# Seven half-size block products for the feature transform of three chunks: an FNet and MLP kernel on one Trainium2 core

## The chip, the cores and the metric

The kernel runs on one core of one Trainium2 chip. The metric is the device time of one execution in microseconds, and lower is better. Engines go by the names of the profile: PE is TensorE (matmuls; PEld is its loading of weights), DVE is VectorE, ACT is ScalarE, POOL is GpSimd, SP is SyncE, which here only issues DMA transfers. Each engine runs its own instructions in order and waits for others by semaphores.

## The reference

The input x has 2048 tokens of 512 features. Four steps run in turn, A, B, A, B; the kernel calls the first A and B layer 0, the second pair layer 1. Cut to what matters here:

```python
def _A_ref(x, dft_seq_re, dft_seq_im, dft_hid_re, dft_hid_im):
    a = jnp.einsum("bsd,ed->bse", x, dft_hid_re)
    b = jnp.einsum("bsd,ed->bse", x, dft_hid_im)
    return jnp.einsum("ts,bse->bte", dft_seq_re, a) - jnp.einsum("ts,bse->bte", dft_seq_im, b)

x = A_x
x = x + _A_ref(_layernorm(x), ...)      # layer A
x = x + _B_ref(_layernorm(x), ...)      # spatial shift and MLP, untouched here
x = x + _A_ref(_layernorm(x), ...)
x = x + _B_ref(_layernorm(x), ...)
```

Step A is a discrete Fourier transform over the tokens and one over the features, of which the real part is kept. The order of the two can be exchanged, and the kernel does the tokens first.

## The kernel before

**Precision.** Every product is done in fp32r, with each operand split into a high and a low part. `mm3` (L315) issues three matmuls per product: high x high (L316), high x low (L317), low x high (L318). The high part is a rounding copy on ScalarE, the low part a subtraction on VectorE.

**Work.** Each of the two A steps handles its 2048 output tokens in four chunks of 512 (NC = 4, `c`). For a chunk, an x phase (`x_phase`, L498) and a y phase (`y_phase`, L531) do the transform over tokens with sums (`ax`) and differences (`ay`) of the normalised input as stationary operand and the DFT matrix `ws` as moving operand, 512 columns at a time, into the PSUM pairs PA, PB, PC, PD. Out come four tiles of features by tokens, `re0`, `re1`, `im0`, `im1`, kept as high and low parts in the region `rr`. The first chunk of layer 0 goes by another routine, `plain_phase` (L456).

**The transform over features** of chunk c - 1 is done inside the x phase of chunk c, by `hid` (L593): eight calls a chunk, two passes over the four blocks of the DFT matrix `hs` (order `HORDER`, L42), each with 2 x 2 products of 128 x 128 by 512 columns into PD. The list `HAT` (L40) puts the calls ahead of the steps k = 2, 3, 3, 4, 5, 5, 6, 6. After four calls `add_y` (L609) adds PD onto two tiles of x (X1) on VectorE, and `y_stats` (L618) takes their statistics. The last chunk's transform runs after the loop over chunks.

**Feeding.** A list `pieces` (L180) of 512 KB blocks is loaded by SP in order into four raw buffers (`issue_dma`, L235; RAW = 4): piece i goes into buffer i mod 4, and waits until the users of piece i - 4 are done. A list `items` (L184) names what TensorE streams, in order. `stage_one` (L247) makes the high part of an item in one of four ring slots (RING = 4): a cast of a plain block on ScalarE (L260), or a difference on VectorE (L262, L266) and then its cast (L263, L267). `stage_two` (L272) makes the low part on VectorE (L279). `stream()` (L304) takes the next item: it frees the slot of the item before, issues the first stage of as many items as have a slot, one low part behind, and returns the slot. In an x phase, each step k has a plain item (12 matmuls) and a "one" item (6); each y item has 12.

**Order around the change.** Everything is issued by hand (`manual_schedule`). `late` is a table of small jobs; `run_late(i)` (L493) issues those of half-step i = 2k or 2k + 1 right behind `stream()` and ahead of that item's matmuls. `hook(i)` does the same for row transfers. In `by_pairs`, which does step B, `D(slot, ...)` and `A(slot, ...)` put jobs on VectorE or ScalarE into numbered slots; at L1050 two sums of z3 blocks stand in slot 26.

Of the kernel before, what the change touches and what calls it, by code (L numbers as in the profile page):

```python
# [40 lines left out]
BACK = {8: 0, 9: 2}  # L41
HORDER = ((1, 0), (0, 1), (1, 1), (0, 0))  # L42


@with_exitstack
def spectral_mlp_kernel(ctx: ExitStack, tc: tile.TileContext, x, ws, hs, w1, w2, w34, out, out_t):
# [40 lines left out]
    EXT = RNG + RING * 4 * CH  # L87
    RAWS = EXT + 6 * D
    STG = RAWS + RAW * 2 * CH
    nc.alloc_sbuf_tensor("arena", [P, STG + 2 * CH], F32)  # L90

# [22 lines left out]
    spare = at("spare", SPARE, 2, D, dtype=F32)  # L114
    (re0, im0), (re1, im1) = ([both(f"rr{i}{h}", RR + (2 * i + h) * 4 * CH, 2, 2, CH) for i in range(2)] for h in range(2))
    rr = [[re0[0], re1[0]], [im0[0], im1[0]]]
    rg = [[at(f"rg{i}{g}", RR + (4 * i + g) * 2 * CH, 2, CH) for g in range(KD)] for i in range(2)]
    ring, ringf = zip(*(both(f"ring{i}", RNG + i * 4 * CH, 2, 2, CH) for i in range(RING)))
# [68 lines left out]
    def y_order():  # L187
        order = [(k, kind) for k in range(NP) for kind in ("by1", "by0")]
        order[-3], order[-2] = order[-2], order[-3]
        return order  # L190

    for layer in range(LAYERS):
        for c in range(NC):
            if layer == 0 and c == 0:
                for k in range(NP):
                    item("plain", piece(ws[c, k][:, 2:4]))
                    item("plain", piece(ws[c, k][:, 0:2]))
                continue
            for k in range(NP):
                if c:  # L200
                    for h in range(NP):
                        if HAT[h] == k:
                            item("plain", piece(hs[HORDER[h % 4]]))
                p = piece(ws[c, k][:, 2:4])
                item("plain", p)
                item("one", p, span=(0, 1))
            ps = [(piece(ws[c, k][:, 2:4]), piece(ws[c, k][:, 0:2])) for k in range(NP)]
            for k, kind in y_order():
                item(kind, *ps[k])
        for o in HORDER:  # L210
            item("plain", piece(hs[o]))
        w_items.append(len(items))
        for i in range(2):
            item("plain", piece(w1[i]), dest=w12[i])
        for i in range(2):
            item("plain", piece(w2[i]), dest=w12[2 + i])
        w_pieces.append(len(pieces))
    users = {}
    for n, it in enumerate(items):
        for i in it[1]:  # L220
            users.setdefault(i, []).append((n, "two" if it[0] == "plain" else "one"))
    raws, slots, sums = {}, {}, {}
    state = {"dma": 0, "one": 0, "two": 0, "use": 0, "made": 0, "done": 0, "limit": 0, "load": w_pieces[0]}
# [11 lines left out]
    def issue_dma(upto=None):  # L235
        while state["dma"] < (state["load"] if upto is None else upto):
            i = state["dma"]
            if i >= RAW and any(n >= state[stage] for n, stage in users[i - RAW]):
                break
            src, a, b = pieces[i]  # L240
            raws[i] = raw_at[i % RAW]
            nc.sync.dma_start(raws[i][:, a:b], src)
            state["dma"] += 1
            if i % 2 and i > 3:
                load_x()
# [198 lines left out]
    re0s, re1s, im0s, im1s = (f[:, :, 1] for _, f in (re0, re1, im0, im1))  # L444
    mid = [rr[i // 2][i % 2].rearrange("p t r (h d) -> p (t r h) d", h=2) for i in range(4)]
    mid = [m[:, 0:4].rearrange("p (i r) d -> p i r d", r=2) for m in mid]

# [8 lines left out]
    def plain_phase(hook):  # L456
# [19 lines left out]
        for (t, _), ps, sign in ((im0, PC, -1.0), (re1, PB, 1.0)):  # L476
            for i in range(2):
                nc.scalar.mul(t[:, i, 0], ps[i], sign)
                nc.vector.scalar_tensor_tensor(
                    t[:, i, 1], ps[i], sign, t[:, i, 0].bitcast(F32), op0=ALU.mult, op1=ALU.subtract  # L480
                )
        for t, ps, sign in ((re0s, PA, 1.0), (im1s, PD, -1.0)):
            for i in range(2):
                nc.scalar.mul(t[:, i], ps[i], sign)
        late[2] = [lambda: high(im1)]
# [7 lines left out]
    def run_late(*names):  # L493
        for i in names:
            for f in late.pop(i, ()):
                f()

    def x_phase(c, hook):  # L498
        h = 0
        for k in range(NP):  # L500
            first, last = k == 0, k == NP - 1
            while c and h < NP and HAT[h] == k:
                s = stream()
                ri, dp = HORDER[h % 4]
                hid(ri, dp, s, PD, 2 * (h // 4), h % 4 == 0, h % 4 == 3)
                if h % 4 == 3:
                    add_y(c - 1, h // 4, PD, X1, 2 * k if h < 4 else 2 * k + 2 if c == NC - 1 else "y")
                hook(NT + h)
                h += 1
# [5 lines left out]
            if last:  # L515
                for i in range(2):
                    nc.scalar.copy(im1s[:, i], PC[i])
                for i in range(2):
                    nc.scalar.copy(re1s[:, i], PB[i])
            s = stream()  # L520
# [3 lines left out]
        for i in range(2):  # L524
            nc.scalar.copy(re0s[:, i], PA[i])

# [4 lines left out]
    def y_phase(c, hook):  # L531
        im = pairs[1] if c == NC - 1 else im0s

# [4 lines left out]
        for k, kind in y_order():  # L538
            first, last = k == 0, k == NP - 1
            s = stream()  # L540
            if kind == "by1":
# [5 lines left out]
                if k == 6 and c == NC - 1:  # L547
                    add(pairs[0], re0s, re1s, ALU.subtract)
                jobs = (PC, ay[k][:, 2], s[:, 0]), (PD, ay[k][:, 0], s[:, 1])
                for job in jobs[::-1] if first else jobs:  # L550
                    mm_half(*job, first, last)
                if last:
                    for i in range(2):
                        nc.vector.scalar_tensor_tensor(
                            im[:, i], PC[i], -1.0, im1s[:, i], op0=ALU.mult, op1=ALU.subtract
                        )
                    nc.scalar.copy(im0[0][:, :, 0], im)
                    if c == NC - 1:
# [3 lines left out]
                    else:  # L562
                        x1_copies()
                    add(im1s, pairs[0] if c == NC - 1 else re0s, im)
            else:
                if k == NP - 2 and c < NC - 1:
                    im0_low(im)
# [7 lines left out]
        for i in range(2):  # L575
            nc.scalar.copy(t[:, 2 + i], PA[i])
        late.update(
            {
                "im1-": [lambda: add(im1s, im1s, re1s, ALU.subtract)] if c < NC - 1 else [],
                "re1+": [lambda: add(re1s, re1s, t[:, 0:2]), lambda: high(re1)],  # L580
                "im1+": [lambda: add(im1s, im1s, X1), lambda: high(im1)],
                "re1": [lambda: low(re1)],
                "re0+": [lambda: add(re0s, re0s, t[:, 0:2])],
                "im1": [lambda: low(im1)],
                "re0++": [lambda: add(re0s, re0s, t[:, 2:4]), lambda: high(re0)],
                "re0": [lambda: low(re0)],
            }
        )
        if c < NC - 1:
            for i, names in enumerate((["im1-"], ["re1+"], ["im1+", "re1"], ["re0+", "im1"], ["re0++"], ["re0"])):  # L590
                late[i + 1] = [f for n in names for f in late.pop(n)]

    def hid(ri, dp, s, acc, t0, first, last):  # L593
        for i in range(2):
            for t, a in enumerate(acc):
                w = slice((t0 + t) * P, (t0 + t + 1) * P)
                mm3(
                    a,
                    rr[ri][dp][:, i, 0, w],
                    rr[ri][dp][:, i, 1, w],  # L600
                    s[:, i, 0],
                    s[:, i, 1],
                    first and i == 0,
                    last and i == 1,
                )
# [231 lines left out]
    def by_pairs(layer, zs, xin, dst):  # L837
# [739 lines left out]
    for layer in range(LAYERS):  # L1577
        xin = x if layer == 0 else x2d
        last_layer = layer == LAYERS - 1
        state["limit"] = w_items[layer]  # L1580
        zs = {}
        for c in range(NC):
            if layer == 0 and c == 0:
                raws[0] = raw_at[0]
                load_x()
# [76 lines left out]
            def hook(i):  # L1662
                k, odd = divmod(i, 2)
                if layer == 0 and c == 1:
                    if i == 1:
                        xp_sums(NP - 1)
# [4 lines left out]
                if c == 0:  # L1671
# [5 lines left out]
                    return  # L1677
                j = (c - 1) * TC
                if i == 4:
                    rows(X1, xin, j, 2, True)  # L1680
# [4 lines left out]
                if c == NC - 1:  # L1685
# [9 lines left out]
                    if i in (14, 15):  # L1695
                        turn_out(turn0, queue=nc.scalar, which=[i - 14])

            x_phase(c, hook)

            def hook(k):  # L1700
                if layer and c == 0 and k == 3:
                    xp_lows(NP - 1, which=slice(1, None))
                if k == 1 and c:
                    rows(X1, x1d, (c - 1) * TC + 2, 2, False)
                if c == NC - 1:
# [94 lines left out]
```

## Time and profile before

| | |
|---|---|
| median of 3 runs | 1429.36 us (1428.56 to 1430.61) |
| profiled execution | 1430.81 us |
| its span, first to last instruction | 1428.8 us |
| busy: PE / DVE / ACT / POOL | 1422.0 / 1147.5 / 726.3 / 79.9 us |
| granted PE clock | 1.0 in the whole span |
| DMA | 302.13 MB, 211 GB/s on average |

A row of the time order reads: start, length, engine, line, operation, what is written and read, sizes; in brackets the idle time of the engine before it and what ended it. A matmul's length is modelled and overlaps the next one's; its pace is read from the starts. A row of a window reads: stretch, its length, busy time of each engine with the number of instructions, PE clock, DMA share and GB/s.

### The profile page before, as it was taken

What the parts mean: (1) busy time and instruction counts of PE and PEld (TensorE: products, weight loads), DVE (VectorE), ACT (ScalarE), POOL (GpSimd) and SP (SyncE); (2) the same over time, 40 slices, a digit from 0 to 9 for tenths busy, and PEclk for the clock granted to TensorE, in tenths of its full rate; (3) what the DMA queues carried; (4) which work ended last, traced back from release to release, by engine and by line L of the source; (5) the groups of instructions that cost most, each with busy time, mean ns of one, the idle gap of its engine ahead of it and who ended that gap; (6) DMA issues with size and microseconds to landing.
All of it is one profiled execution on the core that took longest, in us unless ns stands there. A gap on an engine that the chain in (4) does not pass through costs nothing.

```text
span 1428.8 us, 17276 instructions
## 1 busy us (share of the span) xinstructions
PE 1422.0 (100%) x6258; PEld 1174.2 (82%) x6258; DVE 1147.5 (80%) x1603; ACT 726.3 (51%) x977; POOL 79.9 (6%) x111
## 2 busy tenths in 40 slices
PE   9999999999999999999999999999999999999998
PEld 7888888888888888888888888888888888888887
DVE  7876997988869888677889979888889698637586
ACT  5553454455465745345554544544555576333352
POOL 2100000001002000000000000000000010000000
PEclk9999999999999999999999999999999999999999
DMA  7426646657664859968755566565676468666594
GB/s 243 140 89 207 206 166 203 204 167 245 225 205 111 287 201 321 379 215 319 240 174 195 168 191 204 186 199 190 205 258 225 137 164 303 209 196 260 168 312 144
DMA packets 136813, 302.13 MB, mean 211 GB/s; under 512 B 15372, under 2 KB 61196, under 8 KB 133528
## 3 DMA queue, kind: packets, MB, share of 16 engines
q1 hardware_dynamic: 132504, 298.93, 63.1%
q10 hardware_dynamic: 4224, 2.10, 0.5%
q8 instruction: 49, 0.80, 0.2%
q14 instruction: 36, 0.29, 0.1%
HBM read 246.18 MB, written 54.81 MB: 211 GB/s over the span
## 4 chain that ended last, share of the span: by engine, by line
PE 95%; DVE 3%; DMA 2%; issue 0%; SPq 0%; ACT 0%; DVEq 0%
PE psd L318 10%; PE psd L316 10%; PE psd L317 10%; PE psa L316 9%; PE psa L318 9%; PE psa L317 9%; PE psc L317 6%; PE psc L318 6%; PE psc L316 6%; PE psb L317 6%; PE psb L318 6%; PE psb L316 6%; DMA raw<-in_ws 1%; DVE ring L279 1%; DMA xs<-in_x 1%; DVE ring1f L266 0%
## 5 line engine op out<-in xcount | busy, mean ns | idle before, releaser
L260 ACT CAST ring<-raw 128x1024 fp32r<-128x1024 f32 x127 | 133.0, 1052 | 98.9 <-PE psd L318 50.1
L279 DVE TENSOR_TENSOR ring<-raw,ring 128x1024 fp32r<-128x1024 f32 (+1 forms) x128 | 154.5, 1211 | 22.5 <-ACT ring L260 22.4
L316 PE MATMUL psd<-ring,rr 128*128 128x512 f32 x208 | 80.9, 389 | 0.0
L317 PE MATMUL psd<-ring,rr 128*128 128x512 f32 x208 | 80.9, 389 | 0.0
L318 PE MATMUL psd<-ring,rr 128*128 128x512 f32 x208 | 80.9, 389 | 0.0
L360 POOL TENSOR_TENSOR rs<-ve,mhalf 128x4 f32<-128x4 f32 x16 | 28.7, 1794 | 578.2 <-DVE nm L359 578.2
L267 ACT CAST ring<-ring0f 128x1024 fp32r<-128x1024 f32 x28 | 29.5, 1054 | 57.1 <-DVE ring0f L266 57.1
L279 DVE TENSOR_TENSOR ring<-ring1f,ring 128x512 fp32r<-128x512 f32 (+1 forms) x56 | 53.2, 949 | 0.8 <-ACT ring L263 0.8
L339 POOL TENSOR_TENSOR rs<-ve,mhalf 128x2 f32<-128x2 f32 (+1 forms) x33 | 30.1, 911 | 396.3 <-DVE nb L338 396.3
L317 PE MATMUL psc<-ring,ay 128*128 128x512 f32 x128 | 50.0, 391 | 0.9 <-DVE ring L279 0.9
L317 PE MATMUL psb<-ring,ay 128*128 128x512 f32 x128 | 50.1, 392 | 0.0
L318 PE MATMUL psc<-ring,ay 128*128 128x512 f32 x128 | 49.8, 389 | 0.0
L318 PE MATMUL psb<-ring,ay 128*128 128x512 f32 x128 | 49.8, 389 | 0.0
L316 PE MATMUL psb<-ring,ay 128*128 128x512 f32 x128 | 49.8, 389 | 0.0
L316 PE MATMUL psc<-ring,ay 128*128 128x512 f32 x128 | 49.8, 389 | 0.0
L267 ACT CAST ring<-ring1f 128x1024 fp32r<-128x1024 f32 x28 | 29.5, 1055 | 39.6 <-DVE ring1f L266 39.6
L317 PE MATMUL psa<-ring,ay 128*128 128x512 f32 x126 | 49.0, 389 | 0.0
L316 PE MATMUL psa<-ring,ay 128*128 128x512 f32 x126 | 49.0, 389 | 0.0
L318 PE MATMUL psa<-ring,ay 128*128 128x512 f32 x126 | 49.0, 389 | 0.0
L316 PE MATMUL psd<-ring,ay 128*128 128x512 f32 x126 | 49.0, 389 | 0.0
L317 PE MATMUL psd<-ring,ay 128*128 128x512 f32 x126 | 49.0, 389 | 0.0
L318 PE MATMUL psd<-ring,ay 128*128 128x512 f32 x126 | 49.0, 389 | 0.0
(575 smaller groups left out, 4375.4 us busy)
## 6 DMA issues: line engine op xcount, KB each, us to landing
raw<-in_ws SPq DMA_DIRECT2D x183, 512.0 KB, 4.9
raw<-in_hs SPq DMA_DIRECT2D x56, 512.0 KB, 3.6
w3b<-w3d SPq DMA_DIRECT2D x15, 1792.0 KB, 9.2
w4r<-w4a SPq DMA_DIRECT2D x33, 512.0 KB, 6.0
wq<-w4a SPq DMA_DIRECT2D x22, 512.0 KB, 4.7
w3d<-w3b SPq DMA_DIRECT2D x5, 1792.0 KB, 6.9
x1d<-tmp SPq DMA_DIRECT2D x12, 512.0 KB, 5.8
xs<-x1d SPq DMA_DIRECT2D x12, 512.0 KB, 6.6
```

What stands on the lines that cost most here:

```text
L260: nc.scalar.copy(dest[:, a:b, 0], r[0][:, a:b])
L267: nc.scalar.copy(dest[:, :, 0], lo)
L279: nc.vector.tensor_tensor(lo[:, i], src[:, i], hi[:, i].bitcast(F32), op=ALU.subtract)
L316: nc.tensor.matmul(o, lh, rh, start=first, stop=False, skip_group_check=onto)
L317: nc.tensor.matmul(o, lh, rl, start=False, stop=False, skip_group_check=onto)
L318: nc.tensor.matmul(o, ll, rh, start=False, stop=last, skip_group_check=onto)
L339: nc.gpsimd.tensor_tensor(rs[:, :n], ve[:, :n], mhalf[:, 0, :n], op=ALU.pow)
L360: nc.gpsimd.tensor_tensor(rs, ve, mhalf[:, :, :2], op=ALU.pow)
```

## The change

For three chunks (`by_seven`: the transforms done in the x phases of chunk 2 in layer 0 and of chunks 1 and 2 in layer 1) the 512 x 1024 by 1024 x 512 product becomes seven products of half size, in the manner of Winograd's variant of Strassen's scheme. Each unit (`hid_unit`) has 24 matmuls of 256 columns. The seven moving operands do not depend on the data of the chunk, so they are made once: three of them are stored out of ring slots during the first `hid` calls (layer 0, chunk 1), four are computed in the same x phase (`h_prep`), and all are kept in DRAM (`hd`, 1 MB each) with both parts. The stationary operands are sums and differences of the chunk's own tiles, made by VectorE and ScalarE in the half-steps of `plan_hid`, where the results are collected too. The statistics of the first two tiles and the sum and statistics of the last two move into the y phase (`x1b`). Two raw buffers serve as the buffer `hw[0]` meanwhile, so some pieces (`narrow`) use the other two alone; the region RAWS moves behind STG. The tiles in `rr` are laid out as quarters. Apart from that, one of the two z3 sums goes from slot 26 to slot 27.

```diff
+HUNITS = {3: (0,), 4: (1,), 5: (2,), 6: (3, 4), 7: (5, 6)}
+    hd = [dram.tile([P, KD, 2, 2 * P], F32, name=f"hd{i}") for i in range(7)]
...
+    quarter, quarterf = both("rr", RR, 2, 2, KD, 2, 2 * P)
+    first_diff, first_difff = both("fdiff", EXT, KD, 2, 2 * P)
+    hw = [at("hwa", RAWS + 4 * CH, KD, 2, 2 * P), at("hwb", EXT + 4 * CH, KD, 2, 2 * P), quarter[:, 1, 0]]
+    x1b = at("x1b", RR, 2, D, dtype=F32)
...
+    def by_seven(layer, c):
+        return 1 - layer < c < NC - 1
...
-                if c:
+                if c and not by_seven(layer, c):
                     for h in range(NP):
                         if HAT[h] == k:
                             item("plain", piece(hs[HORDER[h % 4]]))
...
+        j = min(range(2 if i in narrow else RAW), key=lambda j: last_in[j])
...
     def x_phase(c, hook):
+            if seven:
+                for u in HUNITS.get(k, ()):
+                    hid_unit(u)
-            while c and h < NP and HAT[h] == k:
+            while c and not seven and h < NP and HAT[h] == k:
                 s = stream()
                 ri, dp = HORDER[h % 4]
                 hid(ri, dp, s, PD, 2 * (h // 4), h % 4 == 0, h % 4 == 3)
+                if len(at_layer) == 1 and c == 1 and h < KD:
+                    for u, e in ((2, 0), (5, 1)) if h > 1 else ((0, 0),):
+                        v = s.bitcast(F32)[:, :, :, e * 2 * P : (e + 1) * 2 * P]
+                        nc.sync.dma_start(hd[u][:, h % 2 * 2 : h % 2 * 2 + 2], v)
...
+    def h_prep():
...
+        return {
+            2: [load(0), load(1)],
+            3: [load(2), load(3)],
+            5: [total(b22, b12, b22, ALU.add)],
+            6: [total(s2, b22, b11), hi(p, s2)],
+            7: [total(b21, b21, s2)],
+            8: [keep(3, p, s2), total(b12, b11, b12), hi(ka, b12)],
+            9: [keep(4, ka, b12)],
+            10: [hi(p, b22)],
+            11: [keep(1, p, b22)],
+            12: [hi(ka, b21)],
+            13: [keep(6, ka, b21)],
+        }
...
+    HID = (
+        (quarter[:, 0, 0], 1, 0, True),
+        (first_diff, 0, 1, True),
+        (quarter[:, 1, 0], 1, 0, False),
+        (quarter[:, 0, 0], 0, 1, True),
+        (quarter[:, 0, 1], 1, 0, True),
+        (first_diff, 2, 0, False),
+        (quarter[:, 1, 1], 1, 1, True),
+    )
+
+    def hid_unit(u):
+        a, w, b, fresh = HID[u]
+        for part in range(3):
+            for i in range(KD):
+                for t in range(2):
+                    nc.tensor.matmul(
+                        bank_of(PD[b])[:, t],
+                        a[:, i, part == 2, t * P : (t + 1) * P],
+                        hw[w][:, i, part == 1],
+                        start=fresh and part == 0 and i == 0 and t == 0,
+                        stop=part == 2 and i == KD - 1 and t == 1,
+                        skip_group_check=True,
+                    )
+
+    def plan_hid(adds):
...
+        plan = {
+            1: ["im1-", "re1+"],
+            2: ["re0+", hi(q11, a11), load(0)],
+            3: [sub(diff, a21, a11), hi(first_diff, diff)],
+            4: [lo(q11, a11), load(1)],
+            5: ["im1+"],
+            6: [lo(first_diff, diff), "re0++"],
+            7: [evict(v, 0), load(2)],
+            8: [sub(a21, a22, a21), sub(a11, a22, diff), hi(q12, a12)],
+            9: [sub(diff, a12, a11), lo(q12, a12), evict(g, 1), load(3), hi(q11, a11), hi(q21, a21)],
+            10: [lo(q11, a11)],
+            11: [lo(q21, a21), plus(x1_of[:, 0], x1_of[:, 0], d[0]), hi(first_diff, diff), load(4), load(5)],
+            12: [hi(q22, a22), lo(first_diff, diff)],
+            13: [
+                plus(v, v, PD[1]),
+                plus(g, g, v),
+                plus(pairs[0][:, 1], g, PD[0]),
+                lo(q22, a22),
+                plus(x1_of[:, 1], x1_of[:, 1], extra_of[0]),
+                load(6),
+            ],
+            15: [plus(x1_of[:, 1], x1_of[:, 1], d[0]), plus(pairs[0][:, 0], g, PD[1])],
+        }
+        late["x1b"] = [plus(x1b_of, x1b_of, both_halves)]
...
-        D(26, sum_of("t1", "12", "t1"), sum_of("t3", "22", "12"))
+        D(26, sum_of("t1", "12", "t1"))
+        D(27, sum_of("t3", "22", "12"))
...
             def hook(k):
+                if by_seven(layer, c):
+                    if k == 0:
+                        y_stats(j, X1)
+                    if k == 1:
+                        rows(X1, x1d, j, 2, False)
+                        run_late("x1b")
+                    if k == 2:
+                        y_stats(j + 2, x1b)
+                    if k == 3:
+                        rows(x1b, x1d, j + 2, 2, False)
```

In a unit of `HID` stand its stationary tile, the number of its buffer in `hw`, its bank PD[b], and whether it starts the bank afresh; `plus`, `sub` and `lo` are VectorE operations, `hi` and `evict` copies on ScalarE, `load` a DMA from `hd`, and the names in quotes are the adds on `re0`, `re1`, `im1` that were there before.

More of the change, by code (lines that the diff above doesn't have):

```diff
@@ L204, in spectral_mlp_kernel @@
                 p = piece(ws[c, k][:, 2:4])
+                if by_seven(layer, c) and k > 1:
+                    narrow.append(p)
                 item("plain", p)
@@ L221, in spectral_mlp_kernel @@
             users.setdefault(i, []).append((n, "two" if it[0] == "plain" else "one"))
+    place, before = [], []
+    last_in = [-1 - i for i in range(RAW)][::-1]
+    for i in range(len(pieces)):
+        j = min(range(2 if i in narrow else RAW), key=lambda j: last_in[j])
+        place.append(j)
+        before.append(last_in[j])
+        last_in[j] = i
     raws, slots, sums = {}, {}, {}
@@ L237, in issue_dma @@
             i = state["dma"]
-            if i >= RAW and any(n >= state[stage] for n, stage in users[i - RAW]):
+            if before[i] >= 0 and any(n >= state[stage] for n, stage in users[before[i]]):
                 break
             src, a, b = pieces[i]
-            raws[i] = raw_at[i % RAW]
+            raws[i] = raw_at[place[i]]
             nc.sync.dma_start(raws[i][:, a:b], src)
@@ L531, in y_phase @@
     def y_phase(c, hook):
-        im = pairs[1] if c == NC - 1 else im0s
+        im = wide(pairs[1]) if c == NC - 1 else im0s
+        seven = by_seven(at_layer[-1], c + 1)
         def x1_copies():
@@ L547, in y_phase @@
                 if k == 6 and c == NC - 1:
-                    add(pairs[0], re0s, re1s, ALU.subtract)
+                    add(wide(pairs[0]), re0s, re1s, ALU.subtract)
                 jobs = (PC, ay[k][:, 2], s[:, 0]), (PD, ay[k][:, 0], s[:, 1])
@@ L563, in y_phase @@
                         x1_copies()
-                    add(im1s, pairs[0] if c == NC - 1 else re0s, im)
+                    add(im1s, wide(pairs[0]) if c == NC - 1 else re0s, im)
             else:
-                if k == NP - 2 and c < NC - 1:
+                if k == NP - 2 and c < NC - 1 and not seven:
                     im0_low(im)
@@ L591, in y_phase, with load, total, hi @@
                 late[i + 1] = [f for n in names for f in late.pop(n)]
+    def h_prep():
+        ka, kb = (hrawf[:, i] for i in range(2))
+        (b11, b12), (b21, b22) = ([t[:, :, e] for e in range(2)] for t in (ka, kb))
+        p = tmp[:, 0:4].rearrange("p k (r c) -> p k r c", r=2)
+        def load(i):
+            to = (ka, kb)[i // 2][:, i % 2 * 2 : i % 2 * 2 + 2]
+            return lambda: nc.sync.dma_start(to.rearrange("p k r c -> p k (r c)"), hs[HORDER[i]])
+        def total(o, a, b, op=ALU.subtract):
+            return lambda: add(o, a, b, op)
+        def hi(o, src):
+            return lambda: nc.scalar.copy(o[:, :, 0].bitcast(F32R), src)
+        def keep(u, o, src):
+            def f():
+                v = o[:, :, 1].bitcast(F32R)
+                nc.vector.tensor_tensor(v, src, o[:, :, 0], op=ALU.subtract)
+                nc.sync.dma_start(hd[u], o)
+            return f
+        s2 = p[:, :, 1]
+        return {
[11 more added lines that the diff above has]
+        }
@@ new lines, in plan_hid, with load, hi, lo @@
+    def plan_hid(adds):
+        a11, a21, a12, a22 = (quarterf[:, k, h, :, 1] for k in range(2) for h in range(2))
+        diff, sums = (pairs[i].rearrange("p a (b c) -> p (a b) c", b=2) for i in range(2))
+        v, g = (pairs[1][:, i] for i in range(2))
+        x1_of, x1b_of = (wide(t).rearrange("p t h c -> p h t c") for t in (X1, x1b))
+        def load(u):
+            return lambda: nc.sync.dma_start(hw[HID[u][1]].bitcast(F32), hd[u])
+        def hi(o, src):
+            return lambda: nc.scalar.copy(o[:, :, 0], src)
+        def lo(o, src):
+            return lambda: nc.vector.tensor_tensor(o[:, :, 1], src, o[:, :, 0].bitcast(F32), op=ALU.subtract)
+        def sub(o, a, b):
+            return lambda: add(o, a, b, ALU.subtract)
+        def plus(o, a, b):
+            return lambda: add(o, a, b)
+        def evict(o, i):
+            return lambda: nc.scalar.copy(o, PD[i])
+        q11, q21, q12, q22 = (quarter[:, k, h] for k in range(2) for h in range(2))
+        d = [bank_of(p) for p in PD]
+        extra_of = bank_of(v), bank_of(g)
+        plan = {
[20 more added lines that the diff above has]
+            15: [plus(x1_of[:, 1], x1_of[:, 1], d[0]), plus(pairs[0][:, 0], g, PD[1])],
+        }
+        for step, todo in plan.items():
+            late[step] = [adds.get(f, lambda: None) if isinstance(f, str) else f for f in todo]
+        both_halves = pairs[0].rearrange("p h (t c) -> p h t c", t=2)
+        late["x1b"] = [plus(x1b_of, x1b_of, both_halves)]
@@ L1678, in hook @@
                 j = (c - 1) * TC
+                if by_seven(layer, c):
+                    if i == 6:
+                        rows(X1, xin, j, 2, True)
+                    if i == 13:
+                        rows(x1b, xin, j + 2, 2, True)
+                    return
                 if i == 4:
@@ L1696, in hook @@
                         turn_out(turn0, queue=nc.scalar, which=[i - 14])
+            if layer == 0 and c == 1:
+                prep.update(h_prep())
             x_phase(c, hook)
```

77 lines of the change are left out of this document (51 added, 26 removed).

## The prediction

> **What bounds the kernel now.** I read the page first, then the stretches by engine (the windows), then the instructions in order of time around the steps that the change touches.
>
> ```profile
> span 1428.8 us, 17276 instructions
> PE 1422.0 (100%) x6258; PEld 1174.2 (82%) x6258; DVE 1147.5 (80%) x1603; ACT 726.3 (51%) x977; POOL 79.9 (6%) x111
> PE 95%; DVE 3%; DMA 2%; issue 0%; SPq 0%; ACT 0%; DVEq 0%
> ```
>
> ```profile
> 95.04:149.44 54.40, 54.40 (x242) 45.05 (x240) 40.98 (x53) 27.09 (x34) 2.83 (x2) 1.00 0.55 179
> 192.96:247.36 54.40, 54.40 (x242) 45.05 (x241) 44.63 (x54) 26.07 (x32) 2.83 (x2) 1.00 0.56 186
> 247.36:290.88 43.52, 43.52 (x194) 36.04 (x193) 40.25 (x43) 21.33 (x26) 2.23 (x2) 1.00 0.62 201
> ```
>
> TensorE (PE) is busy from end to end and carries 95% of the chain. So every matmul taken out shortens the kernel by its spacing, and every wait put in front of a matmul lengthens it in full. The three stretches are the x phase of layer 0, chunk 1 (where the prepared units will be made), the x phase of layer 0, chunk 2 (one of the three that change) and its y phase. In the columns PE, PEld, DVE, ACT, POOL the point is VectorE (DVE): 44.63 of 54.40 us in the x phase, but 40.25 of 43.52 us in the y phase. Work sent from x to y lands where little room is left. The profiled execution took 1430.81 us, 1.45 above the median of the runs, 1429.36; I add the changes to either.
>
> **Fewer columns on TensorE: the gain.** Before, the transform of one chunk is 8 calls of `hid`, each 2 x 2 x 3 = 12 matmuls of 512 columns: 96. After, it is 7 units of 3 x 4 x 2 = 24 matmuls of 256 columns: 168. Three chunks (layer 0: 2; layer 1: 1 and 2): 288 wide ones go, 504 narrow ones come.
>
> ```profile
> 400.02 0.39 PE L316 MATMUL psb<-ring,rr 128*128 128x512 f32 x1
> ...
> 402.74 0.39 PE L316 MATMUL psb<-ring,rr 128*128 128x512 f32 x1
> ```
>
> Twelve matmuls later is 2.72 us later: 0.2267 us each (0.39 is a modelled length, they overlap). 288 x 0.2267 = 65.3 us go. No narrow matmul at this clock stands in the trace. If spacing goes by columns it is 0.1133 and 504 cost 57.1 (-8.2 us). The other end is the weight load, for each matmul loads its own 128 columns.
>
> ```profile
> 13.53 0.19 PEld L317 LDWEIGHTS psc<-ring,ay 128*128 128x128 f32 x1 [0.92 <-DVE ring L279]
> 13.53 0.50 PE L317 MATMUL psc<-ring,ay 128*128 128x512 f32 x1 [0.49 <-DVE ring L279]
> 13.63 0.19 PEld L318 LDWEIGHTS psc<-ring,ay 128*128 128x128 f32 x1
> 13.87 0.39 PE L318 MATMUL psc<-ring,ay 128*128 128x512 f32 x1
> ```
>
> A load takes 0.19, yet after this wait the next one began 0.10 later: loads can follow each other faster than narrow matmuls would, so I take a spacing near the half, 0.117 (3% for a part that does not shrink with the columns; an estimate): 504 x 0.117 = 59.0, a gain of **6.3 us**. The bounds are 0.1133 and 0.19. These rows also price a wait: after one, the next matmul comes 0.34 later, not 0.227, so each wait costs 0.11 on top.
>
> The Trainium skill (TensorE: Matmul & The Clock Gate, Back-to-back issue gap) gives N/2.4 + 2.5 ns for single warm matmuls: 109 ns at 256 columns, an estimate of -10.3 us. At 512 it gives 216, where this trace has 227.
>
> **A wait in front of unit 5: the largest loss.** Units 4 and 5 share the bank PD[0], and step 13 lets VectorE read the bank between them (`plus(pairs[0][:, 1], g, PD[0])`). Unit 5 follows the six matmuls of that step at once. Where VectorE stands then is to be seen at the same place of before:
>
> ```profile
> 241.92 0.39 PE L316 MATMUL psa<-ring,ax 128*128 128x512 f32 x1
> ```
>
> ```profile
> 238.72 1.37 DVE L491 TENSOR_TENSOR tmp<-psd,tmp 128x512 f32<-128x512 f32 x2 [2.33 <-PE psd L318]
> 240.00 0.68 DVE L262 TENSOR_TENSOR ring3f<-raw 128x512 f32<-128x512 f32 x1
> 240.61 1.22 DVE L279 TENSOR_TENSOR ring<-raw,ring 128x1024 fp32r<-128x1024 f32 x1
> 242.12 1.22 DVE L266 TENSOR_TENSOR ring0f<-raw,raw 128x1024 f32<-128x1024 f32 x1 [0.29 <-PE psb L318]
> 243.26 0.68 DVE L279 TENSOR_TENSOR ring<-ring3f,ring 128x512 fp32r<-128x512 f32 x1
> 243.86 1.22 DVE L266 TENSOR_TENSOR ring1f<-raw,raw 128x1024 f32<-128x1024 f32 x1
> ```
>
> At 241.92 TensorE leaves the wide block of k = 6 and starts its last six matmuls. Only now is the ring slot of that block free, and VectorE, which works in order, waits for it with the first sum of the y phase (L266, 242.12). Its next queued work, one low part, ends the pair at 243.86, 1.94 us after the block. `stream()` issues both ahead of `run_late(13)`, and the four-slot ring has the same distance after the change. Then come three adds of 512: from a bank 0.64 (238.72 to 240.00 for two), from SBUF 0.61 (240.00 to 240.61), and 0.72 until the third has ended: 1.97. The read is over 3.91 after the block; unit 5 was due after 6 x 0.2267 = 1.36. Wait 2.55 + 0.11 = 2.66 us, three times: **+8.0 us**. Nothing covers it: behind unit 5 stand unit 6, the blocks of k = 7 and the whole y phase on the same in-order queue. Unit 6 itself needs only the first of these adds.
>
> **VectorE in the y phase.** After the change the statistics of the first two tiles move to k = 0, the sum of `x1b` is new at k = 1, and the two last adds (1.28) now come behind the first y sums, not at 238.72.
>
> ```profile
> 255.72 1.23 DVE L266 TENSOR_TENSOR ring2f<-raw,raw 128x1024 f32<-128x1024 f32 x1 [0.35 <-PE psd L318]
> ...
> 258.44 1.23 DVE L266 TENSOR_TENSOR ring3f<-raw,raw 128x1024 f32<-128x1024 f32 x1 [0.36 <-PE psa L318]
> ...
> 260.71 1.28 DVE L354 BATCH_NORM_STATS2 st<-tmp 128x6 f32<-128x512 f32 x2
> ...
> 262.46 1.22 DVE L266 TENSOR_TENSOR ring0f<-raw,raw 128x1024 f32<-128x1024 f32 x1
> 263.60 1.22 DVE L279 TENSOR_TENSOR ring<-ring3f,ring 128x1024 fp32r<-128x1024 f32 x1
> ```
>
> Statistics cost 1.75 (260.71 to 262.46), a sum of 1024 costs 1.14 (262.46 to 263.60). Item 7 of the y phase is ready at 264.82 and due at 247.36 + 7 x 2.72 = 266.40, its low part one matmul later: 1.81 spare, plus the idle 0.35 and 0.36 ahead of it: 2.52. New before it: 1.75 + 1.14 + 1.28 = 4.17. TensorE must wait the difference, 1.65 us, per y phase: **+4.9 us** (bounds 0 and 2.5 each, should more of it be spare or the late start be lost twice).
>
> **DMA: units from DRAM.** 24 loads of 512 KB and their 24 casts and low parts go; 21 loads of 1 MB come.
>
> ```profile
> raw<-in_hs SPq DMA_DIRECT2D x56, 512.0 KB, 3.6
> w4a<-w4r SPq DMA_DIRECT2D x11, 512.0 KB, 6.6
> w4s<-w4c SPq DMA_DIRECT2D x5, 1024.0 KB, 4.9
> zt1f<-zd SPq DMA_DIRECT2D x4, 1024.0 KB, 6.2
> ```
>
> Later units have 7 us and more from the release of their buffer. Unit 0 is tight: its load stands in SP's queue behind a raw load, which waits for the low part of the third plain block. That needs the slot of the first narrow block (4.08 + 0.2 after the phase's start), a sum of 0.61 and 1.22: 6.1 at the earliest, some 6.5 with the two adds of step 1. With 4.9 to 6.2 it lands at 11.4 to 12.7; the unit starts at 3 x 18 x 0.2267 = 12.24. I take 0.3 each, **+1 us**, bounds 0 and 3.3. Two raw slots in place of four suffice, since a k step now lasts 7 us and more.
>
> **Making the units, once, in layer 0, chunk 1.** The sums on VectorE (8 x 1.14 = 9.1) fit into the 13 us it idles there. ScalarE's copies at steps 10 and 12 wait until the units stored at steps 8 and 9 have landed; two blocks and two `hid` calls lie between, 42 matmuls or 9.5 us, against 4.9. The stores out of ring slots do not fit: each of the first four `hid` slots may be overwritten only when its store has landed.
>
> ```profile
> 106.16 1.06 ACT L260 CAST ring<-raw 128x1024 fp32r<-128x1024 f32 x1 [1.67 <-PE psd L318]
> ...
> 112.96 1.05 ACT L260 CAST ring<-raw 128x1024 fp32r<-128x1024 f32 x1 [1.17 <-PE psd L318]
> ```
>
> ```profile
> 109.91 2.66 SPq L242 DMA_DIRECT2D raw<-in_hs  x2
> ```
>
> ScalarE refills the slot the moment TensorE leaves it (112.96 for the second). Its store cannot pass the raw loads on SP (the later ends at 112.57), lands 6.6 later at 119.2, then copy and low part: 121.5. TensorE wants that item (the fourth `hid`) at 119.52 + 0.23, so 1.7 us late; at 3.6 to land it would be in time. The first store stands behind four extra loads, the third and fourth slots have two stores each. I take 1.7 for each of the four slots, **+7 us**, bounds 0 and 11.
>
> **The two z3 sums.**
>
> ```profile
> 490.12 0.39 PE L317 MATMUL psd<-w,rg 128*128 128x512 f32 x1
> 490.79 0.50 PE L318 MATMUL psd<-w,rg 128*128 128x512 f32 x1 [0.28 <-DVE rg L701]
> 491.12 0.39 PE L316 MATMUL psd<-w,rg 128*128 128x512 f32 x1
> ```
>
> Two sums ahead of a low part hold TensorE up, 0.67 + 0.33 in place of 0.45. With one moved behind it this goes: **-0.55 us**. The last group, which is late next, is wanted 18 matmuls on.
>
> **Sum**: -6.3 + 8.0 + 4.9 + 1.0 + 7.0 - 0.55 = +14.0. The profiled execution would take 1444.9 us, the median 1443.4.
>
> **Rivals.** (a) *Faster*: VectorE is not late at unit 5. That asks that the read of PD[0] end within 1.36 us of the block, so that the first y sum not stand ahead of it; with the y wait and the stores hidden too, the matmuls' gain and the z3 sum are left: -6.9, or -8.8 at 0.1133: 1420.6 to 1422.5. Against it speaks L266 at 242.12, released by TensorE itself. For it: VectorE has 9.8 us idle in that x phase. (b) *Even*: only the wait at unit 5 is real: -6.3 - 0.55 + 8.0 = +1.1: 1430.5. For it: landings of 3.6 us hide the stores. (c) *Weight loads set the pace*: 504 x 0.19 = 95.8, +30.5 in place of -6.3, and with the wait at unit 5 about 1467. Against it: the 0.10 between two loads at 13.53; for it, that those two matmuls were still wide. The Trainium skill (same page and section) has sustained 131 ns at 512 columns and 81 at 128; read between them, 256 cost 0.75 of 512, an estimate of +20 us for the matmuls. This trace has 227 at 512 columns, not 131.
>
> **How the numbers follow.** The forecast 0.70, (a) 0.12, (b) 0.10, (c) 0.08. Its own range: low, -8.2 + 8.0 - 0.55 = -0.8 (1428.6); high, 0.125 per matmul (-2.3) + 8.0 + 7.5 + 3.3 + 11 - 0.55 = +27 (1456). That takes in (b) and leaves out (a) and (c), 0.20 together. A difference of 0.2%, 2.9 us, is about what a measurement of this kernel can tell from none. Faster by more 0.12 from (a), same 0.10 from (b), slower 0.78 from the forecast and (c).
>
> **What would show it.** Rows of the new unit line with 128x256: their spacing prices the gain (right at 0.113 to 0.120). The first matmul of unit 5 waits some 2.5 us for a DVE add of line `add`, in three places. In the three y phases DVE has no idle time up to item 8 and TensorE waits for L279's successor. In layer 0, chunk 1, ScalarE's casts wait for a DMA of `hd`. The prediction is wrong if unit 5 starts without a wait, or if the narrow matmuls stand 0.13 or more apart.

## The result, and the profile after

The changed kernel takes 1528.1 us in the median (1524.0 to 1533.1, 4 runs) against 1429.5 for the kernel before beside it: 1.069 times as long, 95% interval 1.066 to 1.072. The forecast was 1443.4. The profiled execution took 1527.51 us, 96.7 more than that of before.

The page of the changed kernel: span, busy time, and the chain that ended last.

```profile
span 1525.5 us, 17727 instructions
PE 1447.2 (95%) x6474; PEld 1195.5 (78%) x6474; DVE 1162.3 (76%) x1620; ACT 717.1 (47%) x972; POOL 76.8 (5%) x111
PE 75%; DVE 14%; DMA 5%; issue 3%; ACT 2%; SPq 0%; DVEq 0%; ACTq 0%
```

TensorE carries 75% of the chain where it carried 95%: it waits now, above all for VectorE. Its busy time grew too, though the units bring fewer columns. The windows show why. The stretches are the x phase of layer 0, chunk 1 (which makes the blocks), the x and y phase of chunk 2 (units), and the x phase of chunk 3, which still goes by the old blocks and has nothing new in it.

```profile
96.07:167.97 71.90, 61.00 (x241) 48.07 (x241) 49.92 (x62) 29.86 (x38) 2.23 (x2) 0.91 0.74 258
211.66:279.51 67.85, 55.86 (x314) 49.03 (x312) 45.15 (x49) 26.06 (x34) 0.00 (x0) 0.92 0.61 217
279.51:324.53 45.02, 44.27 (x192) 35.95 (x193) 40.98 (x49) 17.73 (x20) 4.46 (x4) 1.00 0.58 187
324.53:384.28 59.75, 56.78 (x242) 45.99 (x240) 48.79 (x61) 30.41 (x38) 2.83 (x2) 0.97 0.58 189
```

The x phases were 54.40 us each, so +17.5, +13.5 and +5.4; the y phase was 43.52. The last x phase was touched by no step of my sum. The third number from the end, the granted clock, is under 1 in three of the four. TensorE's waits (us in all, times, longest):

```profile
PE psd L700 <- DMA x1b<-x2d: 15.0, 2, 7.5
PE psc L342 <- DVE rrf L522: 13.9, 6, 2.9
PE psd L342 <- ACT ring L286: 8.9, 3, 5.0
PE psd L700 <- DVE rrf L522: 7.9, 3, 2.8
PE psd L700 <- DMA x1b<-in_x: 7.6, 1, 7.6
PE psd L342 <- DVE rrf L522: 6.8, 4, 2.1
PE psd L342 <- DVE tmp L522: 5.4, 3, 1.8
```

The unit line (L700) waits 22.6 us for `x1b`, a load of rows of x that no unit reads. The units of one chunk, each line the 24 matmuls of a unit:

```profile
226.62 3.11 PE L700 MATMUL psd<-hwb,rr 128*128 128x256 f32 x24 [2.56 <-DVE rrf L522]
233.68 3.04 PE L700 MATMUL psd<-hwa,fdiff 128*128 128x256 f32 x24
...
247.64 3.03 PE L700 MATMUL psd<-hwa,rr 128*128 128x256 f32 x24
250.65 3.11 PE L700 MATMUL psd<-hwb,rr 128*128 128x256 f32 x24
265.52 5.22 PE L700 MATMUL psd<-rr,fdiff 128*128 128x256 f32 x24 [7.64 <-DMA x1b<-in_x]
...
279.50 0.47 PE L342 MATMUL psd<-ring,ay 128*128 128x512 f32 x1 [1.79 <-DVE tmp L522]
```

VectorE and then SP in front of unit 5 (265.52), and VectorE in front of unit 0 (226.62):

```profile
259.74 0.69 DVE L522 TENSOR_TENSOR tmp<-tmp,psd 128x512 f32<-128x512 f32 x1
260.34 1.22 DVE L722 TENSOR_TENSOR rr<-rrf,rr 128x1024 fp32r<-128x1024 f32 x1
```

```profile
261.58 0.38 SPq L259 DMA_DIRECT2D x1b<-in_x  x1
```

```profile
225.30 1.22 DVE L522 TENSOR_TENSOR rrf<-rrf,tmp 128x1024 f32<-128x1024 f32 x1
```

The read of PD[0] that I had forecast as the wait of unit 5 is over at 260.4. But the load of `x1b` is issued only when the low part behind it, which belongs to unit 6's tile, ends at 261.56; unit 5 then waits for the load to land. Unit 0 starts when a sum into `im1` ends (225.30 + 1.22), a tile whose half unit 0 does not use.

The common trait: the four tiles were eight names (rr and rrf, the fp32r and fp32 view, for each tile). Now they are one stretch with two names, and `x1b` is a third over some of the same bytes. **Theory A**: between two names the program's order is kept for the whole stretch, so a write to one tile under `rrf` holds up a read of any other under `rr`. **Theory B**, the rival: the new loads, sums and reads really are that late.

A third reading, that a stretch is held as a whole even within one name, is out by the trace of the changed kernel:

```profile
240.66 3.04 PE L700 MATMUL psd<-hwb,rr 128*128 128x256 f32 x24
241.67 2.13 ACT L719 CAST rr<-rrf 128x1024 fp32r<-128x1024 f32 x2 [0.59 <-DVE rr L722]
```

Both casts stand ahead of unit 2 in the program (step 9 against k = 5) and write other tiles of the stretch under `rr`, the name that unit 2 reads. Unit 2 does not wait for them: it starts at 240.66, they at 241.67.

### The profile page after: what moved, and what is told of

It reads as the page before. It is cut to its first block, busy times and chain, and to the rows that moved or that the text cites. A ratio compares the mean times of both kernels' runs of the same rounds, so it can differ in the third digit from the quotient of the medians.

```text
span 1525.5 us, 17727 instructions
## 1 busy us (share of the span) xinstructions
PE 1447.2 (95%) x6474; PEld 1195.5 (78%) x6474; DVE 1162.3 (76%) x1620; ACT 717.1 (47%) x972; POOL 76.8 (5%) x111
## 4 chain that ended last, share of the span: by engine, by line
PE 75%; DVE 14%; DMA 5%; issue 3%; ACT 2%; SPq 0%; DVEq 0%; ACTq 0%
PE psd L342 8%; PE psd L343 8%; PE psd L344 8%; PE psa L342 7%; PE psa L344 7%; PE psa L343 7%; DVE ring L305 5%; PE psc L342 5%; PE psc L343 5%; PE psc L344 5%; PE psb L342 5%; PE psb L343 5%; PE psb L344 5%; PE psd L700 3%; DVE rrf L522 2%
## 5 line engine op out<-in xcount | busy, mean ns | idle before, releaser
L286 ACT CAST ring<-raw 128x1024 fp32r<-128x1024 f32 x103 | 108.0, 1051 | 116.3 <-PE psb L344 36.2
L305 DVE TENSOR_TENSOR ring<-raw,ring 128x1024 fp32r<-128x1024 f32 (+1 forms) x104 | 125.3, 1209 | 29.6 <-ACT ring L286 28.9
L292 DVE TENSOR_TENSOR ring2f<-raw,raw 128x1024 f32<-128x1024 f32 x28 | 34.2, 1221 | 38.4 <-PE psb L344 35.5
L342 PE MATMUL psd<-ring,rr 128*128 128x512 f32 x96 | 40.4, 420 | 15.8 <-ACT ring L286 8.9
L292 DVE TENSOR_TENSOR ring0f<-raw,raw 128x1024 f32<-128x1024 f32 x28 | 34.2, 1221 | 24.4 <-PE psb L344 20.2
L305 DVE TENSOR_TENSOR ring<-ring3f,ring 128x1024 fp32r<-128x1024 f32 (+1 forms) x50 | 49.3, 985 | 2.3 <-ACT ring L289 2.1
L342 PE MATMUL psa<-ring,ay 128*128 128x512 f32 x126 | 49.0, 389 | 0.0
L343 PE MATMUL psa<-ring,ay 128*128 128x512 f32 x126 | 49.0, 389 | 0.0
```

Of the source, the lines that this page charges most:

```text
L286: nc.scalar.copy(dest[:, a:b, 0], r[0][:, a:b])
L292: nc.vector.tensor_tensor(lo, r[1][:, i : i + 1].broadcast_to([P, 2, CH]), r[0], op=ALU.subtract)
L305: nc.vector.tensor_tensor(lo[:, i], src[:, i], hi[:, i].bitcast(F32), op=ALU.subtract)
L342: nc.tensor.matmul(o, lh, rh, start=first, stop=False, skip_group_check=onto)
L343: nc.tensor.matmul(o, lh, rl, start=False, stop=False, skip_group_check=onto)
```

## The experiments

Each is one edit to the changed kernel, or to the run named. In all of them before took 1428.9 to 1429.5 us beside it.

| run | median us | ratio to before (95%) |
|---|---|---|
| e1_layout | 1471.0 | 1.029 (1.027 to 1.031) |
| e2_x1b_later | 1510.1 | 1.057 (1.054 to 1.059) |
| e3_two_names | 1480.7 | 1.036 (1.035 to 1.038) |
| e4_two_layouts | 1469.7 | 1.028 (1.026 to 1.031) |
| e5_reads_early | 1457.9 | 1.020 (1.018 to 1.021) |
| e6_load0_early | 1449.9 | 1.014 (1.013 to 1.016) |
| e7_ring_free | 1467.8 | 1.026 (1.025 to 1.028) |
| e8_z3_alone | 1429.4 | 1.000 (0.999 to 1.001) |
| e9_stats_apart | 1445.4 | 1.012 (1.010 to 1.013) |
| e10_two_chunks | 1441.3 | 1.008 (1.006 to 1.009) |
| e11_spread | 1434.2 | 1.004 (1.002 to 1.005) |
| e12_unit6_hwa | 1431.2 | 1.001 (1.000 to 1.002) |

**e1: the layout without the units.**

```diff
-        return 1 - layer < c < NC - 1
+        return False
```

with the storing and making of blocks taken out.

> No unit products at all: the transform over features goes by its four full blocks in every chunk as before the change, and only the new place of the four tiles (interleaved in one stretch under two names, rr and rrf) and of the raw buffers is kept. Theory A (a tile that is written under rrf holds up a read of another tile under rr, because the order between the two names is kept for the whole stretch and not for the tile): the extra time of the third x phases (+5.0 each) shows in all six x phases that hold the transform, the two last transforms keep their +7.7, so about 1475 us (1460 to 1485) and waits of TensorE on VectorE's L522 in each of them. Theory B (the extra time is the lateness of the new work itself: loads and makes of blocks, reads of PD): 1430 us (1427 to 1434).

1471.0: the layout alone costs 42 us, with no unit in the kernel. Windows of this run, an x phase and the last transform of layer 0 (54.40 and 21.76 before), and its first waits:

```profile
194.28:252.68 58.40, 55.00 (x242) 44.89 (x241) 45.04 (x54) 26.76 (x33) 2.83 (x2) 1.00 0.54 176
401.33:432.29 30.96, 26.88 (x97) 21.17 (x97) 18.56 (x19) 12.71 (x14) 0.21 (x1) 0.85 0.38 126
```

```profile
PE psd L342 <- DVE rrf L522: 17.2, 10, 1.8
PE psc L342 <- DVE rrf L522: 13.9, 6, 2.9
```

Theory B is out as the main cause. Five x phases are 4.0 longer; the two transforms are 9.2 and 7.5 longer, and each starts some 3 us late behind a sum under `rrf`. Together that is the 42 us. The first x phase is not longer (54.6): the chunk ahead of it comes from `plain_phase`, which leaves no sums for later; I had counted six. The interleaved order itself makes the work no slower: a sum onto one of these tiles takes 1219 ns on average in before (first line) and in this run.

```profile
L491 DVE TENSOR_TENSOR rr00f<-rr00f,tmp 128x1024 f32<-128x1024 f32 x10 | 12.2, 1219 | 0.0
L522 DVE TENSOR_TENSOR rrf<-rrf,tmp 128x1024 f32<-128x1024 f32 x22 | 26.8, 1219 | 11.1 <-PE psb L344 11.1
```

**e2: `x1b` loaded behind unit 6.**

```diff
-                    if i == 13:
+                    if i == 14:
                         rows(x1b, xin, j + 2, 2, True)
```

> The load of x1b is issued one step later, behind unit 6 instead of between units 4 and 5; all else as in the changed kernel. Theory A: the fifth unit's wait of 7.5 us goes in the three chunks, with the slow clock behind it; 2 to 3 us of it stay as the wait for PD's read and block 5's own load, and SyncE now holds the y phase's first loads behind unit 6: 1507 us (1500 to 1514). Theory B (unit 5 is late by its own block's load or by VectorE's reads, whatever x1b does): 1524 us or more.

1510.1, 18 us less. Unit 5's 7.6 us become 2.7, the read of PD[0]; unit 5 had needed nothing of `x1b`.

**e3: the same bytes, two tensors.**

```diff
-    quarter, quarterf = both("rr", RR, 2, 2, KD, 2, 2 * P)
+    quarter, quarterf = zip(*(both(f"rr{k}", RR + k * 8 * CH, 2, KD, 2, 2 * P) for k in range(2)))
...
```

> The stretch of the four tiles is two tensors, one for im0 and re1 (and x1b), one for im1 and re0 (and the third unit buffer), at the same addresses; the instructions and their order stay. Theory A: unit 5 no longer waits for x1b (7.5 us in three chunks with the slow clock behind it), unit 0 no longer for the sum of im1 (2.8 in three), and about half of the +5 and +7.7 of the third x phases and last transforms goes: 1487 us (1478 to 1497). Theory B: no change, 1520 us or more.

1480.7, 47 us less with the same instructions in the same order at the same addresses. This is the cleanest evidence for theory A: only which tensor a tile belongs to has changed.

**e4: tiles apart where no units follow.**

```diff
+    layouts = [[whole(j) for j in range(4)], [tile_of(k, m) for k in range(2) for m in range(2)]]
...
+                lay(by_seven(at_layer[-1], c + 1))
```

> As the run with two tensors, and in the chunks whose transform is by four full blocks the tiles stand one behind the other, each a tensor of its own, as before the change; the interleaved order is used ahead of the three chunks with units alone. Theory A: the third x phases, the last transforms and the y phases ahead of them come back to within 1 us of before, and what is left over before is the making of the blocks (about 17 us), the reads of PD ahead of unit 5 and y (3 times 2 to 5) and the y phases: 1462 us (1454 to 1472). Theory B: 1520 us or more.

1469.7: of the 98.6 us, 58 go when the names are apart, with the half pace behind their waits (see the clock below). The third x phase is back, and what is left stands in phases that do new work (the same four stretches as above):

```profile
94.54:164.42 69.88, 60.62 (x242) 47.71 (x240) 48.82 (x60) 29.57 (x36) 2.23 (x2) 0.93 0.77 265
207.96:269.13 61.17, 53.75 (x313) 46.88 (x312) 44.86 (x49) 25.66 (x34) 0.00 (x0) 1.00 0.68 240
269.13:315.02 45.89, 43.92 (x193) 36.05 (x193) 41.00 (x49) 17.75 (x20) 4.47 (x4) 1.00 0.58 183
315.02:369.62 54.60, 54.60 (x241) 44.97 (x240) 48.55 (x61) 30.20 (x38) 2.83 (x2) 1.00 0.63 206
```

Units 0, 4 and 5 and, below, SP and VectorE in e4:

```profile
221.92 3.10 PE L712 MATMUL psd<-hwb,rr 128*128 128x256 f32 x24 [1.55 <-issue]
...
247.39 3.11 PE L712 MATMUL psd<-hwb,rr 128*128 128x256 f32 x24 [1.44 <-DMA hwb<-hd]
257.27 3.10 PE L712 MATMUL psd<-rr,fdiff 128*128 128x256 f32 x24 [2.65 <-issue]
```

```profile
215.13 0.42 SPq L728 DMA_DIRECT2D hwb<-hd  x1
```

```profile
253.29 1.22 DVE L296 TENSOR_TENSOR ring0f<-raw,raw 128x1024 f32<-128x1024 f32 x1 [7.21 <-PE psb L348]
...
256.48 0.69 DVE L533 TENSOR_TENSOR tmp<-tmp,psd 128x512 f32<-128x512 f32 x1
```

Unit 5 starts at 257.27, when the sum of 256.48 has read PD[0]; ahead of that sum VectorE stood idle for 7.21 us and then did the y block that TensorE released. This is the wait of the forecast, 2.8 us from start to start, hidden in the changed kernel behind the larger false one. Unit 0 starts 6.8 us after its load was issued at 215.13.

**e5 and e6, on top of e4: reads and load earlier.**

```diff
             12: [
                 hi(q22, a22),
                 lo(first_diff, diff),
+                plus(v, v, PD[1]),
+                plus(g, g, v),
+                plus(pairs[0][:, 1], g, PD[0]),
             ],
             13: [
-                plus(v, v, PD[1]),
-                plus(g, g, v),
-                plus(pairs[0][:, 1], g, PD[0]),
                 lo(q22, a22),
...
-            15: [plus(x1_of[:, 1], x1_of[:, 1], d[0]), plus(pairs[0][:, 0], g, PD[1])],
+            14: [plus(x1_of[:, 1], x1_of[:, 1], d[0]), plus(pairs[0][:, 0], g, PD[1])],
```

and for e6 `load(0)` at step 0 instead of 2.

> On top of the run with two layouts (1469.7): the three sums that read PD ahead of unit 5 stand one step earlier on VectorE, the two that read PD ahead of the y phase too, so that they no longer queue behind the staging of a block that itself waits for TensorE. Theory C (what is left in those two places is VectorE's order, as the forecast had it for unit 5): the waits of 2.8 us ahead of unit 5 and 2.0 us at the start of y go, three times each, 1456 us (1453 to 1460). Rival D (unit 5 waits for its own block's load, which was issued only after unit 2 and unit 4): under 4 us gained, 1466 or more.

> On top of the run with the early reads: the load of unit 0's block is issued at the start of the x phase and not at its third step. Theory C: unit 0's wait of 1.7 us (three times) goes, 5 us below the run with the early reads, about 1451 us (1447 to 1455). If unit 0 waits for its split operand instead: no change.

1457.9 and 1449.9. Theory C holds for both: the sums used VectorE's idle time, unit 5 no longer waits, and unit 0's load was worth 8.0 us (I had 5). An x phase with units is now about as short as one without (54.21, 54.87 and 53.96 against 54.40).

**e7, on top of e4: no store out of the ring.**

```diff
-            13: [keep(6, ka, b21)],
+            13: [keep(6, ka, b21)] + [lambda u=u: nc.sync.dma_start(hd[u], ka) for u in (0, 2, 5)],
```

> On top of the run with two layouts (1469.7): the three blocks that were stored out of the ring are stored from the buffer of the last difference, all at the end of the phase, so no store holds a ring slot; these three blocks then hold wrong values, the amount moved is the same 1 MB each. Theory E (the making costs what it does because a store holds a ring slot until it lands, and ScalarE's next staging waits for the slot): the first x phase falls from 69.9 to about 56 us, 1456 us (1453 to 1460). Rival F (the added loads, differences and splits on VectorE and ScalarE, or the DMA traffic, make it): the phase stays over 64 us, 1464 or more.

1467.8, outside my range. The three blocks then hold the bytes of another. The phase that makes the blocks did fall, from 69.88 to 56.31, as theory E has it. (The traffic of these stores left that phase too; what tells the ring slots from the traffic is e10, below.) But four stores of 1 MB, issued together, stood ahead of the y phase's loads, VectorE waited 9.44 us for one of these, and what was won in the x phase was lost here (this y phase was 43.5 in e4):

```profile
93.93:150.24 56.31, 55.56 (x242) 44.77 (x240) 47.48 (x59) 28.53 (x34) 2.23 (x2) 1.00 0.75 265
150.24:205.05 54.81, 46.20 (x194) 37.40 (x192) 42.09 (x44) 23.54 (x29) 2.23 (x2) 0.91 0.65 221
```

```profile
165.31 1.23 DVE L296 TENSOR_TENSOR ring0f<-raw,raw 128x1024 f32<-128x1024 f32 x1 [9.44 <-DMA raw<-in_ws]
167.73 0.80 PE L347 MATMUL psb<-ring,ay 128*128 128x512 f32 x1 [7.85 <-DVE ring L309]
```

**e8: the z3 sums alone, on the kernel before.** Its edit is the last one of the change.

> The kernel before with nothing but the two sums on z3 blocks a slot apart: 0.5 us faster (0 to 1), not to be told from no change in the whole, to be seen in the length of the first layer's second half (313.9 instead of 314.5 us).

No difference in the whole. The second half of layer 0, from the trace of before and of e8:

```profile
411.58:726.03 314.45, 314.17 (x1382) 258.73 (x1380) 247.07 (x437) 170.43 (x261) 18.60 (x34) 1.00 0.74 255
```

```profile
411.05:725.01 313.96, 313.90 (x1381) 259.13 (x1380) 247.32 (x437) 170.39 (x261) 18.54 (x34) 1.00 0.75 256
```

0.49 us less there, as forecast (0.55), in one execution each.

**e9, on top of e6: the statistics apart.** `y_stats(j, X1)` moves from k = 0 of the y phase to step 15 of the x phase (and the store of these rows from k = 1 to k = 0), `y_stats(j + 2, x1b)` from k = 2 to k = 4.

> On top of the run with early reads and load (1449.9): the statistics of the first two rows move out of the y phase to the end of the x phase ahead of it, those of x1b two blocks later in the y phase. Theory C (the y phases are longer because VectorE, with 4.9 of each 5.4 us taken there, also has two statistics and a sum in its first half): the three y phases, together 5.1 us over before, come to within 2 us, 1446.5 us (1444 to 1449). If the y phases are late by their loads: no change.

1445.4. The three y phases are 43.6, 44.2 and 44.2 us (in e6 44.4, 46.1, 45.1, before 43.52): 3.6 of the 5.0 us over before went, so VectorE's room was most of the limit there.

**e10, on top of e9: two chunks, blocks made one at a time.**

```diff
-        return 1 - layer < c < NC - 1
+        return layer and 0 < c < NC - 1
```

and `h_prep` spread over two x phases of layer 0, from raw blocks, with no store out of the ring.

> On top of that: units in the two chunks of the second layer alone, and the seven blocks made out of the raw blocks in SBUF, one at a time over the first layer's second and third x phases, none out of the ring. What theories A, C and E leave: the gain of two chunks (2 times 1.6), the z3 sums 0.5, against 2.8 us of waits for loads of blocks 4 and 6, 1 us in the y phases and 0 to 2 us of making: 1430 us (1427 to 1434), so no better than before by more than can be measured. If the making costs by its traffic or its splits wherever it stands: the first layer's second and third x phases stay 5 us or more over 54.4 each, 1440 or more.

1441.3, outside my range. The first of these phases makes three blocks and stores two of them within it, out of `tmp`. It loses nothing (54.40) at a DMA rate of 255 GB/s, where e4's had 265: so neither the splitting nor the traffic holds TensorE up by itself, and the ring slots are left as the cause of what e7 won. The next phase, where four sums and differences stood in its first steps beside the sums left from the chunk before, is late by VectorE, and the units' phases still wait for the last block's load (54.40, 43.52 and 54.40 before):

```profile
192.76:252.49 59.73, 56.22 (x242) 44.42 (x240) 51.40 (x60) 27.89 (x34) 2.23 (x2) 1.00 0.64 212
252.49:298.55 46.06, 44.87 (x194) 35.66 (x192) 41.52 (x44) 22.58 (x27) 2.23 (x2) 1.00 0.68 228
809.79:866.45 56.66, 54.80 (x314) 48.77 (x312) 44.20 (x49) 23.51 (x30) 0.00 (x0) 0.97 0.72 255
```

**e11 and e12: these two cured.** e11 moves the sums and differences behind step 6 and the last two blocks into the x phase after; e12 loads the last unit's block half a step earlier, keeps two more raw blocks out of its buffer, and has

```diff
-        (quarter[1][:, 1], 1, 1, True),
+        (quarter[1][:, 1], 0, 1, True),
```

> On top of the run with two chunks (1441.3): the differences and splits of the last four blocks stand clear of the six steps in which VectorE still has the sums of the chunk before: two blocks in the second half of the first layer's third x phase, two in its fourth. If its 5.3 us over 54.4 and the 2.6 us of the y phase behind it are VectorE's crowding in those steps: both phases to within 1.5 us of before, 1434.5 us (1432 to 1438). If they are the stores' traffic: no less than 1439.

> On top of the spread making: the last unit's block goes to the first unit buffer, free after unit 3, instead of the second, free only after unit 4, and the next pair of raw blocks is kept out of it until then. If the last unit's wait of 2 us in both chunks, with the slow clock of 1.4 us behind it, is that load's landing: 6 us below the run with the spread making, 1429 us (1426 to 1433), which no measurement would tell from before. If the next raw blocks come late in their stead: up to 3 us of wait at the start of the y phases, 1432 or more.

1434.2 and 1431.2, both inside their ranges, though e12 gained 3.0 us of the 6 that I had expected: in e11 the last unit's waits were 1.9 and 0.4, with no half pace behind them, so there was less to win. In e12 the making costs 0.1 us in the phase that cost 5.3 in e10, and each units' phase is 1.2 to 1.3 us shorter than before:

```profile
192.73:247.24 54.51, 54.51 (x242) 45.00 (x241) 50.56 (x60) 28.09 (x34) 2.23 (x2) 1.00 0.65 204
803.40:856.47 53.07, 53.07 (x314) 47.25 (x313) 43.92 (x48) 23.53 (x30) 0.00 (x0) 1.00 0.74 266
900.54:953.70 53.16, 53.12 (x314) 47.24 (x313) 43.96 (x48) 23.78 (x31) 0.00 (x0) 1.00 0.66 232
```

That is near all that two chunks can give (2 times 1.6), and scattered waits of 0.2 to 1.1 us, most of them in y phases, take it back: no version run here beats before. Three chunks with blocks made in time were not tried.

## Why the prediction was wrong, point by point

The direction was right, the size far off: neither 1528.1 nor e4's 1469.7 lies within 1428.6 to 1456.0. I compare the terms in e4, where the names are out of the way and 40 us are left; the bold numbers are what that run (e8 for the z3 sums) gives for each, and they add up to 39.5. The sum had 14.0, so without the names, too, it was 25.5 short. Neither sign of being wrong that I had named came up: the narrow matmuls stand 0.120 apart, and in e4 unit 5 waits for the read of PD[0].

- **The failed step: the layout at no cost.** That the tiles are "laid out as quarters" got neither a term nor a bound in my sum. It was 58 us (1528.1 less 1469.7), and e1 shows 42 of that kind without one unit. The rows of before could not show it, since there each tile has names of its own; the diff could: `both("rr", ...)` in place of four, and `x1b` and `hw[2]` over the same stretch.
- **Narrow matmuls, -6.3.** The trace has 22 of a unit's 24 spacings at 0.120 us: 504 x 0.120 = 60.5 against 65.3, **-4.8**. Rival (c), weight loads at 0.19, is out. The Trainium skill (TensorE: Matmul & The Clock Gate, Back-to-back issue gap) gave estimates of 0.109 by its single warm matmuls, and of 0.170 by its sustained pace (0.75 of 0.227); 0.120 is nearer to the first.
- **Unit 5 on the read of PD[0], +8.0.** 2.8 us three times, **+8.4**, by the cause given, so rival (a) is out: right, but not to be seen until the wait for `x1b` was taken away.
- **y phases, +4.9.** **+4.5** in e4, 5.0 in e6, for the most part for the reason given, as e9 shows. What I had not seen is the read of PD at step 15: the y phase's first matmul goes to PD and waits for it, 1.95 three times, **+5.8**. I had charged those adds to VectorE's queue alone.
- **Unit 0's load, +1.0 (0 to 3.3).** 1.7, 1.9 and 2.1 us, **+5.7**, and **1.4** of slow clock behind one. I let the load be issued at 6.5 after the phase's start and land 4.9 to 6.2 later; in e4 it left at 7.2 and the unit started 6.8 after that. A load of block 4 that waits for its buffer until unit 2 is done was missed: 1.6, 1.2, 0.7, **+3.5**.
- **Making, +7 (0 to 11).** **+15.5** (69.88 less 54.40). The mechanism held (e7: ring slots held by stores), but the changed kernel's trace shows ScalarE waiting 11.90 and 5.85 us at two slots (and 1.74 at a third) where I had TensorE 1.7 late at each of four:

```profile
117.92 1.04 ACT L286 CAST ring<-raw 128x1024 fp32r<-128x1024 f32 x1 [11.90 <-DMA hd<-ring]
129.65 1.04 ACT L286 CAST ring<-raw 128x1024 fp32r<-128x1024 f32 x1 [5.85 <-DMA hd<-ring]
```

- **z3 sums, -0.55.** **-0.5** in e8.
- **The clock, in no term.** I priced a wait at its length and 0.11. In the changed kernel, matmuls at 0.427 in place of 0.227 (or 0.213 in place of 0.120) add up to some 16 us; in before there are none, in e4 5 us, in e11 none. So some 11 of the 58 us are half pace behind the false waits.

## What to carry to other kernels

When a change puts several tiles under one name, or a new buffer over old ones, list which writes then stand ahead of which reads by name alone, and price that like any wait: here it was three fifths of the loss. A large false wait hides the true ones behind it, so take the waits out one by one before you judge the terms. A store that reads a slot of a short ring holds the slot until it has landed, and what the ring does not cover of that stops the engines (15.5 us here); a pile of stores ahead of loads that are due does the same (11.3 us in e7's y phase).

## What the hardware showed that I had not expected

After a wait TensorE may run at about half pace for some us, but the length of the wait alone does not decide it. In e4 the 2.65 us ahead of unit 5 were followed by a unit of 3.10 us, full pace. The last unit of the same chunk waited 1.86 us in e10 and ran at half pace for most of its length (4.60, first line); in e11 it waited 1.88 us and ran at full pace (3.10):

```profile
857.90 4.60 PE L721 MATMUL psd<-hwb,rr 128*128 128x256 f32 x24 [1.86 <-DMA hwb<-hd]
851.54 3.10 PE L720 MATMUL psd<-hwb,rr 128*128 128x256 f32 x24 [1.88 <-DMA hwb<-hd]
```

The Trainium skill (TensorE: Matmul & The Clock Gate, What's actually happening) has the clock drop to one half after an idle window of about 3.4 us, counted by a window that runs freely. Half pace agrees with 0.427 against 0.227; that 1.86 us suffice does not agree with a whole idle window, and the measurement decides. That the window's position explains why 2.65 us did nothing, and 1.88 us in e11, is my reading; no run tested it.
